# A causal convolution followed by an ELU feed-forward block: the tap band read unreversed from DRAM, an earlier halo memset, and a weight chunk copied inside SBUF

## The chip, the cores and the metric

The kernel runs on one core of one Trainium2 chip. The metric is the device time of one execution in microseconds (us), and smaller is better. Beside it there is one profiled execution, whose trace gives the start and length of every instruction, the releases of semaphores and the DMA records. TensorE is called PE here, VectorE DVE, ScalarE ACT, GpSimd POOL and SyncE SP, as in the profile.

## What is computed

The input `x` is 8 sequences of 4096 tokens of 192 channels. Each of the 8 heads (24 channels each) has 7 taps; the taps go through a softmax and then form a causal convolution along the sequence. The result goes through a two-layer block with an ELU between the layers.

```python
w = np.exp(weight - weight.max(-1, keepdims=True)); w /= w.sum(-1, keepdims=True) + 1e-9
x_pad = np.concatenate([np.zeros((B, 6, D)), x], axis=1)       # six zero tokens before each sequence
out = np.einsum('hk,bskhg->bshg', w, x_unf)                      # x_unf: 7-token windows of x_pad
h = out.reshape(32768, 192) @ w_in                               # 192 x 2048
g = np.where(h > 0, h, np.exp(np.minimum(h, 0)) - 1)
y = g @ w_out                                                    # 2048 x 192
```

## The kernel before, in words

The 32768 tokens are cut into 32 supers of 1024 tokens, four to a sequence. For every super, 16 steps (`q`, one per 128 columns of `w_in`) are made, 512 steps `n` in all. A step has two halves `u` (512 tokens each), which sit in the two 64-row halves of the PE array.

For each step and half, PE makes three matmuls into a PSUM bank of `H` (line 751: `w_in` against `att`, the convolved tokens), ACT takes the exponential into `E` (543), POOL clamps it (471), DVE forms `gT` as the maximum of `E - 1` and `H` and so frees the bank (612). Later PE makes the second product from `gT` and `w_out` (785). The bank pool for `H` has six places, so PE can be three steps ahead of DVE and no more. An order of all PE instructions is written out by the planner at the top (`put`, `steps`), with assumed costs; the other engines walk through the same list.

The convolution of a super is done on PE too (line 729), as matmuls of tokens `xg` with a band matrix `Tm` (128 partitions, 8 heads, 128 columns) that holds the seven taps of a head along its diagonals. ACT evicts it to `csb` (521), and SP turns it into `att` by a DMA transpose (389). Super 0 takes another way at the start: its tokens are loaded in fp32, cast, transposed on PE and convolved with diagonal matrices `Dg` (580, 684), so that step 0 need not wait for the band. The matmuls for super 1 stand in the PE order at steps 7 to 10 (`EARLY_CONV`), those for super 2 from step 13. Short "warm" matmuls (701) stand beside steps 0 to 5.

The band is made as follows. DVE writes the softmaxed taps into eight rows `zt` of 128 elements (570). SP writes two zero rows (802) and these eight rows (807) into a DRAM tensor `conv_taps`, waits for both, and reads 128 partitions of 1024 elements from it, each partition one element further than the one before (811), into `Tr`. DVE then copies `Tr` with each head's 128 elements reversed into `Tm` (598). In the DVE program this copy stands ahead of the first `gT`, and in the PE program the first convolution matmul waits for it (`s_tm`), and for the two tokens loads of super 1 (`x_ready`).

POOL issues the large loads at the start, in this order (line 475 on): `w_in` columns 0 to 511 for both partition halves (the same rows go to partitions 0 to 63 and 64 to 127), columns 512 to 2047 for both halves, `xg` of super 1 in two parts, `w_out`, `xg` of super 2 in two parts. All of these cast fp32 to 16 bits on the way. `Q_PART` says which chunk's semaphore PE waits for at a step.

A sequence begins at every fourth super, and its first six rows of `xg` must be zero. `pad_x(s)` on POOL (409, 410) does that with a memset, two supers ahead, at step `X_PAD` = 8 of the super, ahead of that step's clamps. The convolution of super `s + 2` begins in the PE order at step 9 of super `s`.

Of the kernel before, what the change touches and what calls it, by code (L numbers as in the profile page):

```python
# [8 lines left out]
BF16 = mybir.dt.bfloat16  # L9
# [3 lines left out]
P = 128  # L13
HP = 64
FC = 128
D = 192
HEADS = 8
KSIZE = 7
CPH = 24
CW = 128  # L20
# [4 lines left out]
TAP = 6  # L25
# [9 lines left out]
    ((0, (0, 15, 8, 9)), (1, (6, 6, 7, 13))),  # L35
)
RUN = 4
WCOLS = ((0, 512), (512, 2048))
Q_PART = (0,) * 4 + (1,) * 12
WARM = (9, 1)  # L40

CONV_AT = ((0, 1, 1, 0), (4, 1, 1, 1), (9, 2, 0, 0), (12, 2, 0, 1))
# [4 lines left out]
QUAD = 4  # L47
XTW = 136
HALO = 2
X_PAD, X_COPY, X_LOAD = 8, 3, 15  # L50
X_LATE = (13, 18)


def bass_lightweight_conv__then__act_elu_kernel(
# [94 lines left out]
    for n in range(NP):  # L149
        s, i = divmod(n, NQ)  # L150
# [64 lines left out]
            t, half = divmod(n_half - 1, 2)  # L215
            previous[n_half // 2, n_half % 2, 0, g] = (t, half, 0, g)

    taps = nc.dram_tensor("conv_taps", ((HEADS + 2) * CW,), BF16).ap()

    xb = nc.dram_tensor("x_cast", (NT, D), BF16).ap()  # L220

    with ExitStack() as stack:
        def sbuf(name, shape, dt):
            return stack.enter_context(nc.sbuf_tensor(name, shape, dt))
# [4 lines left out]
        def sema(name):  # L229
            return stack.enter_context(nc.semaphore(name))  # L230
# [9 lines left out]
        whe = sbuf("whe", [HEADS, KSIZE], FP32)  # L240
# [1 line left out]
        whr = sbuf("whr", [HEADS, 1], FP32)  # L242
        sel = sbuf("sel", [HEADS, P], BF16)
        xg = sbuf("xg", [P, NXB, 2 * WPG, D], BF16)
        Tr = sbuf("Tr", [P, HEADS, CW], BF16)
        Tm = sbuf("Tm", [P, HEADS, CW], BF16)
        csb = sbuf("csb", [P, 2, 3 * 2 * WPG * HP], BF16)
        att = sbuf("att", [P, 2, 3, WPG * TOK], BF16)
        w_in = sbuf("w_in", [P, 3, FF], BF16)
# [4 lines left out]
        zt = sbuf("zt", [HEADS, CW], BF16)  # L254
        xf = sbuf("xf", [P, 2, QUAD, D], FP32)
        zw = sbuf("zw", [P, GS], BF16)
        scr = sbuf("scr", [P, 2], FP32)
        H = psum("H", [P, 3, 2 * GS])
        ops = psum("ops", [P, 2, GS])

        s_w = [sema(f"s_w{i}") for i in range(3)]
        s_wd = sema("s_wd")
        s_xl = [sema(f"s_xl{i}") for i in range(2)]
        s_xh = sema("s_xh")
        s_xha = sema("s_xha")
        s_wp = sema("s_wp")
        s_wb = sema("s_wb")
        s_tm = sema("s_tm")
        s_xb = [sema(f"s_xb{i}") for i in range(2)]
        s_xq = [[sema(f"s_xq{i}_{g}") for g in range(2)] for i in range(NXB)]  # L270
        s_id = sema("s_id")
# [23 lines left out]
        s_band = sema("s_band")  # L295
# [98 lines left out]
        @block.gpsimd  # L394
        def _gpsimd(g: bass.BassGpSimd):
            W = Waits(g)

            def load_x(s, part):
                g.dma_start(  # L399
                    xg[:, s % NXB, WPG * part : WPG * (part + 1), :],  # L400
                    bass.AP(
                        tensor=x_flat.tensor,
                        offset=(s * SUP + GS * part - PAD) * D,
                        ap=[[D, P], [TOK * D, WPG], [1, D]],
                    ),
                ).then_inc(s_x[s % NXB][part], 16)

            def pad_x(s):
                x_ready(W, s, 0)
                g.memset(xg[0:PAD, s % NXB, 0, :], 0.0).then_inc(s_z)  # L410

            def copy_x(s):
                W(s_cv, 4 * (s - NXB - 1) + 1)
                if s == NXB + 1:
                    g.dma_start(  # L415
                        xb[s * SUP - 8 : s * SUP, :], x_flat[s * SUP - 8 : s * SUP, :]
                    ).then_inc(s_xb[s % 2], 16)
                g.dma_start(  # L418
                    xb[s * SUP : (s + 1) * SUP, :].rearrange("(p t) d -> p (t d)", p=P),
                    x_flat[s * SUP : (s + 1) * SUP, :].rearrange("(p t) d -> p (t d)", p=P),  # L420
                ).then_inc(s_xb[s % 2], 16)

            def load_w_in(k, halves):
                c0, c1 = WCOLS[k]
                for r in halves:
                    g.dma_start(  # L426
                        w_in[HP * r : HP * (r + 1), :, c0:c1],
                        moe_w_in.rearrange("(p j) f -> p j f", j=3)[:, :, c0:c1],
                    ).then_inc(s_w[k], 16)

            W(s_one, 1)
            g.affine_select(
                out=ident[:],
                in_=ident[:],
                pattern=[[-1, P]],
                compare_op=ALU.is_equal,
                fill=0.0,
                base=0,
                channel_multiplier=1,
            ).then_inc(s_id)  # L440
            g.affine_select(
                out=sel[:].rearrange("p (r h c) -> p r h c", r=2, h=HEADS),
                in_=sel[:].rearrange("p (r h c) -> p r h c", r=2, h=HEADS),
                pattern=[[0, 2], [-1, HEADS], [0, 8]],
                compare_op=ALU.is_equal,
                fill=0.0,
                base=0,
                channel_multiplier=1,
            ).then_inc(s_id)
            W(s_wd, 16)  # L450
            load_w_in(0, (0, 1))
            load_w_in(1, (0, 1))
            load_x(1, 0)
            load_x(1, 1)
            g.dma_start(
                w_out.rearrange("p (q r) d -> p q (r d)", r=RUN),
                moe_w_out.rearrange("(q p r) d -> p q (r d)", p=FC, r=RUN),
            ).then_inc(s_w[2], 16)
            load_x(2, 0)
            load_x(2, 1)  # L460
            for n in range(NP):
                s, i = divmod(n, NQ)
                if i == X_PAD and s + 2 < NS and (s + 2) % SPB == 0:
                    pad_x(s + 2)
                if i == X_COPY and s and s + 3 < NS:
                    copy_x(s + 3)
                if n == X_LATE[0]:
                    copy_x(3)
                for u in range(2):
                    W(s_exp, 2 * n + u + 1)  # L470
                    g.tensor_scalar(  # L471
                        out=E[:, n % NE, u, :],
                        in0=E[:, n % NE, u, :],
                        scalar1=1.0,
                        scalar2=0.0,
                        op0=ALU.min,
                        op1=ALU.max,
                    ).then_inc(s_clp)
# [72 lines left out]
        def _vector(v):  # L551
            W = Waits(v)
# [16 lines left out]
            W(s_v, 4)  # L569
            v.tensor_scalar(  # L570
                out=zt[:, TAP : TAP + KSIZE],
                in0=whe[:],
                scalar1=whr[:, 0:1],
                scalar2=None,
                op0=ALU.mult,
# [4 lines left out]
            v.tensor_tensor(  # L580
                Dg[:, 1:8, :],
                mask[:, :].unsqueeze(1).to_broadcast([P, KSIZE, HP]),
                H[:, 2, 0:KSIZE].unsqueeze(2).to_broadcast([P, KSIZE, HP]),
                ALU.mult,
            ).then_inc(s_D)
            W(s_tp, 3)
# [7 lines left out]
            v.tensor_copy(  # L594
                att[:, 0, 2, GS // 2 : GS], H[:, 1, GS : GS + GS // 2]
            ).then_inc(s_hd)
            W(s_band, 48)
            v.tensor_copy(Tm[:], Tr[:, :, ::-1]).then_inc(s_tm)  # L598
            for x_, op in enumerate(steps):
                if x_ in stops:  # L600
                    acc = acc_of(op)
# [3 lines left out]
                elif op[0] == "h" and op[3] == 2:  # L605
                    n, u = op[1:3]
                    s, q = divmod(n, NQ)
                    if s >= NG3:
# [5 lines left out]
                        in0=E[:, n % NE, u, :],  # L614
# [7 lines left out]
        def _tensor(pe):  # L622
            W = Waits(pe)
# [51 lines left out]
            for j in range(3):  # L675
# [3 lines left out]
                for k in range(KSIZE + 1):  # L679
                    shift, i = divmod(k - PAD, QUAD)  # L680
                    step = 2 * XTW if i < 2 else 1 - 2 * XTW
                    for r in range(2):
# [5 lines left out]
                                tensor=whole.tensor,  # L688
                                offset=whole.offset,
                                ap=[whole.ap[0], [step, 2], [1, P]],  # L690
# [7 lines left out]
            for x_, op in enumerate(steps):  # L698
# [10 lines left out]
                elif op[0] == "c":  # L709
# [3 lines left out]
                    if hh == 0 and second:  # L713
                        W(s_cs, 2 * m + b + 1)
                    elif hh == 0:
                        if m == 0:
                            W(s_tm, 1)
                            if b:
                                W(s_cv, 1)
                        for part in range(2):  # L720
                            x_ready(W, s, part)
                        W(s_z, z_need[s])
                        if m >= OPS_CONV:
                            wait_bank()
                        elif m:
                            W(s_ce, 2 * (m - 1) + b + 1)
                    n1 = BN // HB
                    h = 4 * u + HB * b + hh
# [12 lines left out]
                elif op[0] == "h":  # L741
                    _, n, r, j = op
                    s, q = divmod(n, NQ)
# [1 line left out]
                        W(s_ha, (1, 1, 2)[j])  # L745
                        W(s_hd, (0, 1, 2)[j])
                    if j == 0:
                        W(s_w[Q_PART[q]], 32)
                        W(s_att[s % 2], 16 * ((s + 1) // 2))
                        wait_bank()  # L750
                    ins = pe.matmul(  # L751
# [13 lines left out]
                else:  # L765
                    _, item, rt, g = op
                    t, half, q, kb, turned = item
                    acc = acc_of(op)
                    W(s_w[2], 16)
                    W(s_tt, 2 * (NQ * t + q) + g + 1)  # L770
                    at_end = acc[:2] == (last, 1)
                    if x_ in begins:
# [24 lines left out]
        def _sync(sy):  # L797
            W = Waits(sy)
# [1 line left out]
            load_first(sy, 1)  # L800
            W(s_zw, 1)
            sy.dma_start(
                bass.AP(tensor=taps.tensor, offset=0, ap=[[(HEADS + 1) * CW, 2], [1, CW]]),
                zw[0:2, 0:CW],
            ).then_inc(s_band, 16)
            W(s_wp, 1)
            sy.dma_start(
                bass.AP(tensor=taps.tensor, offset=CW, ap=[[CW, HEADS], [1, CW]]), zt[:, :]
            ).then_inc(s_band, 16)
            W(s_band, 32)  # L810
            sy.dma_start(
                Tr[:, :, :].rearrange("p h e -> p (h e)"),
                bass.AP(tensor=taps.tensor, offset=TAP + 1, ap=[[1, P], [1, HEADS * CW]]),
            ).then_inc(s_band, 16)

            def load_cast(s):
                W(s_cv, 4 * (s - NXB))
# [16 lines left out]
            for x_, op in enumerate(steps):  # L834
                if op[0] == "h" and op[2:] == (0, 0):
                    s, i = divmod(op[1], NQ)
# [52 lines left out]
```

## Time and profile before

| | |
|---|---|
| median of three runs | 734.09 us (733.89 to 734.24) |
| profiled execution, whole / its span | 735.32 us / 733.0 us |
| PE busy | 717.8 us (98% of the span) |
| ACT, DVE, POOL busy | 657.2, 652.7, 630.5 us (90, 89, 86%) |
| first matmul of step 0 (751) | starts at 10.95 us |
| `Tr` read (811), issue to the last of its landings | 7.27 to 16.29 us |
| first `gT` (612) | starts at 16.65 us |
| first convolution matmul (729) | starts at 23.74 us |
| first second-layer matmul (785) | starts at 32.12 us |
| halo memsets (410) | 7, of 0.25 us each |

PE is busy in every slice of the page but the first, so a microsecond in which PE stands still late in the kernel is a microsecond of the total. In the first 32 us this isn't so yet: PE has no second-layer work, and the time of a step is that of the slowest engine in the ring PE, ACT, POOL, DVE, or of a load. Times in the text are counted from the start of the span.

### The profile page before, as it was taken

To read this page: it belongs to the slowest core of one execution; us is meant where nothing else is said; L and a number is where in the kernel's file an instruction comes from. 1 tells how busy PE (TensorE), PEld (TensorE's weight loads), DVE (VectorE), ACT (ScalarE), POOL (GpSimd) and SP (SyncE) were. 2 spreads that over 40 slices of the span, in tenths; PEclk is the share of its full clock that TensorE was granted. 3 is DMA by queue.
4 is the path that set the end of the run, shared out by engine and by line. 5 is a ranking of instruction groups with operands and counts; after the bars stand their busy time and mean duration, and the time that the engine had idled before them with its cause. 6 is when DMAs were issued, how large, how long until landed. Compare 5 with 4: busy or idle time off the path is not lost.

```text
span 733.0 us, 28722 instructions
## 1 busy us (share of the span) xinstructions
PE 717.8 (98%) x11866; PEld 640.9 (87%) x11866; DVE 652.7 (89%) x1044; ACT 657.2 (90%) x1286; POOL 630.5 (86%) x1076
## 2 busy tenths in 40 slices
PE   6999999999999999999999999999999999999997
PEld 3598999888999898998998989998898989898997
DVE  3899899999999899998999999999899999999994
ACT  4898999989999999999999989999999989999993
POOL 6889888888888898888898888898888888888893
PEclk9899999999999999999999999999999999999999
DMA  9755334445445544335554445464345453532212
GB/s 177 110 93 114 70 93 115 103 81 98 86 94 114 91 92 106 78 94 114 89 95 99 86 94 114 84 100 97 81 99 115 80 104 86 100 93 70 57 36 66
DMA packets 128959, 69.12 MB, mean 94 GB/s; under 512 B 93932, under 2 KB 127596, under 8 KB 128364
## 3 DMA queue, kind: packets, MB, share of 16 engines
q1 hardware_dynamic: 123596, 52.04, 30.3%
q0 software_dynamic: 4944, 14.75, 14.4%
q8 instruction: 93, 1.52, 0.9%
q10 hardware_dynamic: 288, 0.49, 0.2%
q14 instruction: 38, 0.31, 0.1%
HBM read 43.51 MB, written 36.57 MB: 109 GB/s over the span
## 4 chain that ended last, share of the span: by engine, by line
PE 94%; DMA 2%; ACT 2%; POOL 1%; issue 1%; DVE 0%; ACTq 0%
PE ops L785 50%; PE H L751 40%; PE H L729 3%; DMA Tr<-conv_taps 1%; ACT E L543 1%; POOL E L471 1%; PE H L785 1%; DMA conv_taps<-zt 0%; DVE gT L612 0%; POOL xg L410 0%; ACT L484 0%; ACT csb L521 0%; PE ops L701 0%; POOL x_cast L415 0%; POOL x_cast L418 0%
## 5 line engine op out<-in xcount | busy, mean ns | idle before, releaser
L612 DVE SCALAR_TENSOR_TENSOR gT<-E,H 128x512 f16<-128x512 f32 x1024 | 646.5, 683 | 59.9 <-POOL E L471 51.2
L471 POOL TENSOR_SCALAR E<-E 128x512 f32<-128x512 f32 x1024 | 607.0, 616 | 90.2 <-ACT E L543 86.4
L543 ACT ACTIVATE E<-H 128x512 f32<-128x512 f32 x1024 | 566.8, 613 | 58.3 <-PE H L751 53.8
L751 PE MATMUL H<-att,w_in 64*128 64x512 bf16 x3072 | 612.2, 379 | 5.1 <-DVE gT L612 4.3
L785 PE MATMUL ops<-w_out,gT 64*128 64x192 f16 x8064 | 594.6, 243 | 0.0
L785 PEld LDWEIGHTS ops<-w_out,gT 64*128 64x128 f16 x8064 | 523.7, 94 | 41.6 <-PE ops L785 26.2
L751 PEld LDWEIGHTS H<-att,w_in 64*128 64x128 bf16 x3072 | 293.1, 111 | 20.3 <-DVE gT L612 7.6
L729 PE MATMUL H<-xg,Tm 64*128 64x240 bf16 x480 | 87.6, 262 | 4.1 <-POOL xg L410 3.8
L521 ACT ACTIVATE csb<-H 128x480 bf16<-128x480 f32 x120 | 70.5, 588 | 0.0
L513 ACT ACTIVATE osb<-ops 128x384 f32<-128x384 f32 x125 | 61.1, 488 | 7.3 <-PE ops L785 5.7
L729 PEld LDWEIGHTS H<-xg,Tm 64*128 64x128 bf16 x480 | 39.7, 94 | 19.0 <-issue 6.6
L418 POOL DMA_DIRECT2D x_cast<-in_x_dram x29 | 15.7, 540 | 0.0
L785 PE MATMUL H<-w_out,gT 64*128 64x192 f16 x128 | 6.5, 243 | 0.0
L785 PEld LDWEIGHTS H<-w_out,gT 64*128 64x128 f16 x128 | 5.8, 94 | 0.0
L701 PE MATMUL ops<-zw 64*128 64x512 bf16 x12 | 5.7, 502 | 0.0
L598 DVE COPY Tm<-Tr 128x1024 bf16<-128x1024 bf16 x1 | 0.4, 427 | 5.7 <-DMA Tr<-conv_taps 5.7
L640 PE MATMUL ops<-zw 128*128 128x512 bf16 x9 | 4.0, 631 | 1.3 <-DVE zw L553 1.3
L604 DVE COPY osb<-ops 128x384 f32<-128x384 f32 x1 | 0.6, 558 | 4.3 <-PE ops L785 4.3
L640 PEld LDWEIGHTS ops<-zw 128*128 128x128 bf16 x9 | 1.2, 142 | 3.2 <-issue 1.9
L399 POOL DMA_DIRECT2D xg<-in_x_dram x4 | 3.5, 877 | 0.0
L729 PE MATMUL ops<-xg,Tm 64*128 64x240 bf16 x16 | 3.0, 265 | 0.4 <-ACT csb L521 0.3
L426 POOL DMA_DIRECT2D w_in<-in_moe_w_in_dram x4 | 2.7, 682 | 0.3 <-DMA wh<-in_weight_dram 0.3
(50 smaller groups left out, 30.6 us busy)
## 6 DMA issues: line engine op xcount, KB each, us to landing
out_dram<-osb SPq DMA_DIRECT2D x126, 192.0 KB, 3.2
x_cast<-in_x_dram POOLq DMA_DIRECT2D x29, 384.0 KB, 5.1
xg<-x_cast SPq DMA_DIRECT2D x58, 192.0 KB
xg<-x_cast SPq DMA_DIRECT2D x58, 26.2 KB
w_in<-in_moe_w_in_dram POOLq DMA_DIRECT2D x2, 576.0 KB, 11.7
xg<-in_x_dram POOLq DMA_DIRECT2D x4, 240.0 KB, 15.3
w_out<-in_moe_w_out_dram POOLq DMA_DIRECT2D x1, 768.0 KB, 16.4
att<-csb SPq DMA_TRANSPOSE x31, 5.9
```

Source lines behind the costliest of these rows:

```text
L399: g.dma_start(xg[:, s % NXB, WPG * part : WPG * (part + 1), :], bass.AP(tensor=x_flat.tensor, offset=(s * SUP + GS * part - PAD) * D, ap=[ ...
L418: g.dma_start(xb[s * SUP : (s + 1) * SUP, :].rearrange("(p t) d -> p (t d)", p=P), x_flat[s * SUP : (s + 1) * SUP, :].rearrange("(p t) d - ...
L471: g.tensor_scalar(out=E[:, n % NE, u, :], in0=E[:, n % NE, u, :], scalar1=1.0, scalar2=0.0, op0=ALU.min, op1=ALU.max,).then_inc(s_clp)
L513: a.activation(*out_pieces(acc), ACT.Copy).then_inc(s_oev)
L521: return a.activation(csb[:, s % 2, :].rearrange("p (j v h i) -> p h j v i", j=3, v=2 * WPG, h=HEADS)[:, h0 : h0 + HB], bank_of(("c", m, b ...
L543: a.activation(E[:, n % NE, u, :], bank_of(op[:3]), ACT.Exp).then_inc(s_exp)
L612: v.scalar_tensor_tensor(out=gT[:, s % NG3, q, u, :], in0=E[:, n % NE, u, :], scalar=1.0, in1=bank_of(op[:3]), op0=ALU.subtract, op1=ALU.m ...
L640: pe.matmul(ops[:, 0, :], zw[:, 0:P], zw[:], start=True, stop=True)
L701: pe.matmul(ops[:, 1 - rt, :], zw[HP * rt : HP * (rt + 1), 0:P], zw[HP * rt : HP * (rt + 1), :], start=True, stop=True, tile_position=(HP ...
L729: ins = pe.matmul(bank_of(op[:3])[:, n1 * hh : n1 * (hh + 1)], Tm[HP * rt : HP * (rt + 1), h, :], xg[HP * rt : HP * (rt + 1), s % NXB, :, ...
L751: ins = pe.matmul(bank_of(op[:3]), w_in[HP * r : HP * (r + 1), j, RUN * FC * (q // RUN) + q % RUN : RUN * FC * (q // RUN + 1) : RUN,], att ...
L785: ins = pe.matmul(to[:, d0 : d0 + D], gT[HP * rt : HP * (rt + 1), t % NG3, q, g, t0 : t0 + P], w_out[HP * rt : HP * (rt + 1), q, :], start ...
```

## The change

- The taps are written into `zt` in reversed order, and `Dg` reads them back in reversed order. `conv_taps` holds the zero rows and tap rows twice, one copy behind the other. The band is read straight into `Tm`, and each partition starts one element before the one before it; partitions 64 to 127 read from the second copy. `Tr`, its copy on DVE and `s_tm` are gone; PE waits for the band's own semaphore.
- `X_PAD` is 5 in place of 8.
- `w_in` comes in three chunks. Columns 1024 to 2047 are loaded from DRAM for partitions 0 to 63 only, ahead of columns 512 to 1023; SP then copies them inside SBUF to partitions 64 to 127, behind the band read. At steps 8 to 15 PE waits for the load (rows 0 to 63) or the copy (rows 64 to 127).

```diff
-WCOLS = ((0, 512), (512, 2048))
-Q_PART = (0,) * 4 + (1,) * 12
+WCOLS = ((0, 512), (512, 1024), (1024, 2048))
+Q_PART = (0,) * 4 + (1,) * 4 + (2,) * 8
-X_PAD, X_COPY, X_LOAD = 8, 3, 15
+X_PAD, X_COPY, X_LOAD = 5, 3, 15
...
-    taps = nc.dram_tensor("conv_taps", ((HEADS + 2) * CW,), BF16).ap()
+    taps = nc.dram_tensor("conv_taps", (2 * (HEADS + 2) * CW,), BF16).ap()
...
             load_w_in(0, (0, 1))
+            load_w_in(2, (0,))
             load_w_in(1, (0, 1))
...
-                in0=whe[:],
+                in0=whe[:, ::-1],
...
-                H[:, 2, 0:KSIZE].unsqueeze(2).to_broadcast([P, KSIZE, HP]),
+                H[:, 2, KSIZE - 1 :: -1].unsqueeze(2).to_broadcast([P, KSIZE, HP]),
...
-            W(s_band, 48)
-            v.tensor_copy(Tm[:], Tr[:, :, ::-1]).then_inc(s_tm)
...
-                            W(s_tm, 1)
+                            W(s_band, 48)
...
-                        W(s_w[Q_PART[q]], 32)
+                        if Q_PART[q] < 2:
+                            W(s_w[Q_PART[q]], 32)
+                        else:
+                            W(s_wc if r else s_w[2], 16)
...
-                bass.AP(tensor=taps.tensor, offset=0, ap=[[(HEADS + 1) * CW, 2], [1, CW]]),
-                zw[0:2, 0:CW],
+                bass.AP(tensor=taps.tensor, offset=0, ap=[[(HEADS + 2) * CW, 2], [(HEADS + 1) * CW, 2], [1, CW]]),
+                zw[0:2, 0 : 2 * CW].rearrange("p (a e) -> p a e", a=2),
...
-                bass.AP(tensor=taps.tensor, offset=CW, ap=[[CW, HEADS], [1, CW]]), zt[:, :]
+                bass.AP(tensor=taps.tensor, offset=CW, ap=[[CW, HEADS], [(HEADS + 2) * CW, 2], [1, CW]]),
+                zt[:, :].unsqueeze(1).to_broadcast([HEADS, 2, CW]),
...
-                Tr[:, :, :].rearrange("p h e -> p (h e)"),
-                bass.AP(tensor=taps.tensor, offset=TAP + 1, ap=[[1, P], [1, HEADS * CW]]),
+                Tm[:, :, :].rearrange("p h e -> p (h e)"),
+                bass.AP(tensor=taps.tensor, offset=CW + TAP + KSIZE - 1, ap=[[(HEADS + 2) * CW - HP, 2], [-1, HP], [1, HEADS * CW]]),
             ).then_inc(s_band, 16)
+
+            c0, c1 = WCOLS[2]
+            W(s_w[2], 16)
+            sy.dma_start(w_in[HP:P, :, c0:c1], w_in[0:HP, :, c0:c1]).then_inc(s_wc, 16)
```

More of the change, by code (lines that the diff above doesn't have):

```diff
@@ L244, in bass_lightweight_conv__then__act_elu_kernel @@
         xg = sbuf("xg", [P, NXB, 2 * WPG, D], BF16)
-        Tr = sbuf("Tr", [P, HEADS, CW], BF16)
         Tm = sbuf("Tm", [P, HEADS, CW], BF16)
@@ L259, in bass_lightweight_conv__then__act_elu_kernel @@
         ops = psum("ops", [P, 2, GS])
-        s_w = [sema(f"s_w{i}") for i in range(3)]
+        s_w = [sema(f"s_w{i}") for i in range(4)]
+        s_wc = sema("s_wc")
         s_wd = sema("s_wd")
@@ L267, in bass_lightweight_conv__then__act_elu_kernel @@
         s_wb = sema("s_wb")
-        s_tm = sema("s_tm")
         s_xb = [sema(f"s_xb{i}") for i in range(2)]
@@ L457, in _gpsimd @@
                 moe_w_out.rearrange("(q p r) d -> p q (r d)", p=FC, r=RUN),
-            ).then_inc(s_w[2], 16)
+            ).then_inc(s_w[3], 16)
             load_x(2, 0)
@@ L768, in _tensor @@
                     acc = acc_of(op)
-                    W(s_w[2], 16)
+                    W(s_w[3], 16)
                     W(s_tt, 2 * (NQ * t + q) + g + 1)
```

## The prediction

> **What bounds the kernel now.** I read the page's busy shares first (PE 98%), then the waits of the whole run for what stops PE, then the chain of waits and equal stretches for what each stop costs. Two places stand out. The waits, with columns engine, line, who was waited for, total us, times, longest:
>
> ```profile
> PEld H L751 <- DVE gT L612: 7.6, 8, 4.2
> ...
> DVE Tm L598 <- DMA Tr<-conv_taps: 5.7, 1, 5.7
> ...
> PE H L729 <- POOL xg L410: 3.8, 7, 0.6
> ```
>
> The first two belong together: DVE stands before the band copy, so it frees no bank of `H`, so PE stands. The third is the halo memset, seven times.
>
> The chain of the start (start, length, what) and stretches cut at PE's clock changes (length, busy us with instruction counts, granted clock, DMA share, GB/s):
>
> ```profile
> 3.61 3.64 DMA conv_taps<-zt
> ...
> 7.27 9.02 DMA Tr<-conv_taps
> ...
> 16.31 0.43 DVE Tm L598
> 16.74 0.61 DVE gT L612
> ...
> 17.39 1.64 PE H L751 x5
> ```
>
> ```profile
> 13.28:16.69 3.41, 0.43 (x5) 0.00 (x0) 0.38 (x2) 1.56 (x4) 2.71 (x5) 1.00 1.30 199
> 16.69:20.10 3.41, 2.71 (x13) 1.62 (x15) 3.41 (x7) 1.20 (x2) 0.53 (x1) 0.50 1.32 206
> 20.10:23.52 3.42, 3.42 (x20) 2.37 (x17) 2.70 (x5) 2.39 (x4) 2.43 (x5) 0.50 1.38 196
> 23.52:26.93 3.41, 3.26 (x31) 1.84 (x28) 3.04 (x5) 3.08 (x7) 3.04 (x6) 1.00 0.32 38
> ```
>
> PE stands from 13.7 to 17.39, then runs 6.8 us at half clock, and reaches the first convolution at 23.74. The token loads of super 1 landed at 18.35 and 19.68 by the landing records, so here they delay nothing.
>
> Around a halo memset, the chain, and stretches of one super each (the first and last hold a memset):
>
> ```profile
> 71.42 0.62 POOL E L471
> 72.03 0.20 POOL xg L410
> 72.23 0.24 issue
> 72.48 0.26 PE H L729
> ```
>
> ```profile
> 141.27:164.00 22.73, 22.18 (x375) 19.83 (x372) 20.46 (x33) 20.57 (x41) 19.73 (x35) 1.00 0.47 93
> 164.00:185.83 21.83, 21.83 (x371) 19.68 (x368) 20.10 (x33) 20.30 (x41) 19.35 (x34) 1.00 0.50 96
> 185.83:207.74 21.91, 21.91 (x372) 19.78 (x370) 20.19 (x33) 20.37 (x41) 19.45 (x34) 1.00 0.49 97
> 207.74:229.65 21.91, 21.91 (x372) 19.79 (x370) 20.19 (x33) 20.38 (x41) 19.44 (x34) 1.00 0.49 97
> 229.65:252.38 22.73, 22.18 (x375) 19.82 (x372) 20.47 (x33) 20.57 (x41) 19.73 (x35) 1.00 0.48 93
> ```
>
> PE is full but for 0.55 us in each super with a memset.
>
> **What the Trainium skill says.** "TensorE: Matmul & The Clock Gate", Part 1: the clock halves after about one idle window of 3.4 us in a free-running grid, and returns after a busy one. The trace agrees: two stretches of 3.41 us at 0.50, after one that PE spent almost wholly idle. "DMA: Bandwidth & Descriptors", Why a DMA increments its semaphore by 16: a DMA issued by SP runs on k engines, the largest number up to 16 that divides the slowest dimension of both access patterns, and the other 16 - k counts are written at once. The trace agrees: the band's semaphore shows 28 increments, 2 + 1 for the two zero rows, 8 + 1 for the eight tap rows, 16 for the 128-partition read. Same page, Queues, rings and completion order: an engine takes turns between the queues that have work, and one queue keeps its order. The trace agrees: from 11 to 14 us 116 band rows (2 KB, mostly 96 ns) and 145 `w_in` rows (3 KB, 248 ns) went side by side, about one to one.
>
> **Part 1, the halo.** Four supers take 22.73 + 21.83 + 21.91 + 21.91 = 88.38 us, against 4 x 21.91 = 87.64 without the memset: 0.74 each (the stall of 0.55 and what follows it). Seven times: 5.2 us, at least 7 x 0.55 = 3.8. Is it hidden at step 5? The memset stands ahead of clamps that start at 68.30 there (72.20 now), after 0.25 us in which POOL is idle: it fits. The rows it writes landed at 59.97 (first case) and 146.9 (second, clamps at 156.7), so POOL won't block; if it did, PE would run dry after its three banks, some 4 us. The convolution is at 72, 3.6 us after the new place. I take -5.0.
>
> **Part 2, the band and the loads, up to the first convolution.** DVE's first clamped `E` is there at 13.1 (POOL starts it at 12.49, 0.62 us), so without the copy `gT` starts 3.55 us sooner and PE doesn't stop at 13.7. A step then costs two `gT`, 1.28 us; PE needs the bank freed by the first half of step 4, and so stands before the first convolution at 13.1 + 4 x 1.28 + 0.64 = 18.9. What does it wait for there?
>
> The new read's source has an outermost dimension of 2, its target 128. By the skill's rule k is 2: 64 rows on each of two engines where there were 8. No DMA before shows this shape with this size, so I work out the load on these two engines and bound it.
> - Start: issued near 7.3 to 7.6 as now (the tap writes have one more 256-byte row of 31 ns per engine). The first rows moved 3.5 us after issue, behind a `w_in` transfer; now 10.0 to 10.8.
> - `w_in` work per engine after chunk 0: before 24 rows of 3 KB, 24 x 248 = 5.95 us. After: 12 of 2 KB (173 ns, between the 97 of 1 KB rows and 248) and 24 of 1 KB (97 unhindered, 146 at the pace seen from 4 to 8 us): 4.4 to 5.6, so 0.4 to 1.6 less.
> - The band: 64 x 96 - 8 x 96 = 5.4 us more.
> - The SBUF copy: 12 rows of 2 KB, 12 x 96 = 1.15 us more, on these engines behind the band.
>
> Sum for the two: 5.4 + 1.15 less 0.4 to 1.6, so 5.0 to 6.2, say 5.5 more. The second token load's typical engines landed at 17.4 to 18.2, so on these two it lands near 23.1 (22.4 to 24.4). Five of 16 engines ran nearly 2 us later (19.0 to 19.7); if one of them is among the two, near 24.9 (24.0 to 25.9). The band itself is done earlier, as it takes turns with loads that end later. With even odds the convolution begins at 24.0 (22.4 to 26).
>
> The stall from 18.9 is hidden by nothing. `w_in` columns 512 to 1023, now third, land at about 15 to 17.6, wanted at step 4 (15.0); that only moves part of the same stall forward. The copied half chunk, wanted a step after the convolution begins, lands with the tokens. `w_out` (23.4 now) and super 2's tokens (26.0) come about 5 us later on the two engines, 28.5 and 31; wanted at 32.0 and 31.9. SP's next job is the transpose at 30.73: nothing is queued behind the copy.
>
> After the convolution begins, ACT is the bound (busy 6.02 of the 6.07 us from 26.93). It now starts step 7's first exponential at about 24.9; after, 0.5 us behind the convolution, 1.0 at half clock (a stall of 5 us may hold a whole idle window). So break-even is a convolution at 24.4, or 23.9 at half clock; with 24.0 I get -0.4 or +0.1. I take -0.2, with the ends -2 (22.4) and +2.1 (26 at half clock).
>
> The reversed operands of DVE (0.22 and 0.61 us) keep their sizes. If a reversed read cost double, `Dg` still has 1.1 us before PE's use at 7.37, and the taps add 0.22 to the band's start. I take 0. The copy's 0.43 us is in the 3.55.
>
> **Sum.** -5.0 - 0.2 = -5.2: span 733.0 to 727.8, that execution 735.32 to 730.1, and, as it lies 1.2 above the median, 728.9 for the median.
>
> **The rivals.**
> - *The start keeps its gain*: the read is spread over 16 engines. Then the tokens land near 19.7 as now, the convolution starts by 20.2 (20.7 for the exponential against 24.9): -4.2, total 734.09 - 5.0 - 4.2 = 724.9. For it: nothing in the trace but that this shape is new. Against: the 2 + 1 and 8 + 1 increments. 0.13.
> - *One of the two engines is a late one and the clock halves*: start +1.5 to +3.5, total 730.6 to 732.6. Five late of 16 speak for it; that the stall is shortened by the step-4 wait, against. 0.20.
> - *Another wait takes the memset's place*: at the convolution of a new sequence PE would wait as long for a bank or a load. Total 733.9, no change. The other three supers show no wait at that place. 0.06.
> - *The band rows go slowly on two engines*: slower than before. Single rows took up to 294 ns in crowded moments. It decides where the start loses more than 5.0 + 1.5: 6.8 us over 64 rows, from about 205 ns a row. At 250: 64 x 154 ns = 9.9, total about 738.5. Against: 96 ns was the usual length with 16 engines at it. 0.08.
>
> **How the numbers follow.** The forecast case, start within -1.5 and +1.5, halo -5.0, has 0.53 and 727.4 to 730.6. A difference of 0.2% is 1.5 us and is about what can be told from no change. Faster is 0.53 + 0.13 + 0.20 = 0.86, the same 0.06, slower 0.08. The range 725.0 to 732.6 leaves out the lower half of the first rival and the last two, 0.2 in all.
>
> **What would show it.** Halo: the wait of 729 on the memset gone, all supers at 21.9. Start: no PE stop at 13.7; first `gT` at 13.1; a PE stop of 4 to 6 us that ends with the first convolution at 23 to 25; 2 + 1 increments for the band; its rows moving until after 19 us. Wrong would be: the band landed by 15 (then 724.9), or the convolution after 28.

## The result and the profile after

The changed kernel takes 731.54 us in the median (731.19 to 731.63), against 734.14 before (now the median of four runs, with a later one): a ratio of 0.9964 with a 95% interval of 0.9947 to 0.9981. The forecast was 728.9, so about half of the forecast gain (2.6 of 5.2 us) came. That is outside the forecast case's own 727.4 to 730.6 and inside the wider range, which reached up to 732.6 for a rival. The profiled execution took 731.6 us, with a span of 729.1.

The waits of the whole run after (engine, line, who was waited for, total us, times, longest). The convolution's line is now 727, the first product's 752, the second's 786:

```profile
PEld H L752 <- DVE gT L610: 5.7, 13, 0.8
...
PEld ops L727 <- issue: 5.4, 2, 5.2
PE ops L727 <- DMA xg<-in_x_dram: 5.0, 1, 5.0
...
PE H L727 <- DVE gT L610: 0.3, 1, 0.3
```

The wait of 729 on the halo memset (3.8 us, 7 times) is gone, and so is the long stop behind DVE. In its place PE waits 5.0 us, once, for the tokens of super 1. The chain of waits at the start says the same (start, length, what):

```profile
5.77 0.90 POOL xg L398
6.67 17.07 DMA xg<-in_x_dram
23.74 0.14 issue
23.87 0.36 PE ops L727
```

A load of 240 KB takes 17 us. The reason is in the landing records of the trace; each landing is one DMA engine's increment of a semaphore (times in us):

```
                          before                     after
band read                 16 landings, 13.9-16.3     2 landings, 20.83 and 21.45
tokens of super 1, part 2 16 landings, 17.4-19.7     14 landings, 14.8-17.0, and 22.92 and 23.74
copy inside SBUF          -                          14 landings, 19.9-21.2, and 22.75 and 23.41
```

On 14 engines the tokens are there by 17.0; on the two others, where the band read is, they come 6 to 7 us later. The stretches after, cut in part where the clock changes (length, busy us with counts for PE, PEld, DVE, ACT and POOL, granted clock as a share of PE's full one, DMA share, GB/s):

```profile
15.10:18.50 3.40, 3.21 (x23) 1.23 (x22) 3.40 (x7) 2.94 (x6) 3.40 (x7) 1.00 1.18 252
18.50:21.67 3.17, 0.42 (x4) 0.11 (x1) 2.94 (x5) 1.08 (x2) 1.95 (x4) 1.00 1.31 221
21.67:25.08 3.41, 1.21 (x9) 0.95 (x10) 0.00 (x0) 0.00 (x0) 0.00 (x0) 0.50 0.63 82
25.08:28.50 3.42, 3.36 (x22) 2.02 (x19) 1.28 (x2) 2.76 (x6) 1.73 (x3) 0.50 0.17 24
28.50:33.00 4.50, 3.92 (x28) 1.50 (x25) 3.85 (x6) 4.50 (x10) 3.65 (x8) 1.00 0.03 3
```

DVE now runs through the time in which it stood before the band copy. But PE stops at 18.9, five microseconds later than it did before, and for longer, and comes back at half clock. The first second-layer matmul starts at 33.22 us, against 32.12 in the profile before.

Two stretches of one super each, of which the first ends and the second begins just ahead of a halo memset's place, show what the memset now costs:

```profile
134.50:156.40 21.90, 21.90 (x373) 19.75 (x370) 20.18 (x33) 20.36 (x42) 19.37 (x34) 1.00 0.45 97
156.40:178.30 21.90, 21.90 (x373) 19.75 (x369) 20.17 (x33) 20.37 (x42) 19.57 (x35) 1.00 0.50 97
```

PE has no gap in either. The 0.2 us more of POOL in the second is the memset, and nobody waits for it.

### The profile page after: what moved, and what is told of

It reads as the page before. It is cut to its first block, busy times and chain, and to the rows that moved or that the text cites. A ratio compares the mean times of both kernels' runs of the same rounds, so it can differ in the third digit from the quotient of the medians.

```text
span 729.1 us, 28725 instructions
## 1 busy us (share of the span) xinstructions
PE 715.9 (98%) x11866; PEld 638.9 (88%) x11866; DVE 651.5 (89%) x1043; ACT 656.2 (90%) x1286; POOL 629.0 (86%) x1077
## 4 chain that ended last, share of the span: by engine, by line
PE 95%; DMA 2%; POOL 1%; ACT 0%; DVE 0%; issue 0%
PE ops L786 51%; PE H L752 40%; PE H L727 3%; DMA xg<-in_x_dram 2%; PE H L786 1%; POOL E L471 0%; POOL w_in L425 0%; ACT E L543 0%; DVE gT L610 0%; PE ops L727 0%; POOL xg L398 0%; ACT csb L521 0%; POOL x_cast L414 0%; POOL x_cast L417 0%; POOL sel L440 0%
## 5 line engine op out<-in xcount | busy, mean ns | idle before, releaser
L727 PEld LDWEIGHTS ops<-xg,Tm 64*128 64x128 bf16 x16 | 1.5, 114 | 6.8 <-issue 5.4
L699 PE MATMUL ops<-zw 64*128 64x512 bf16 x12 | 4.2, 379 | 0.0
## 6 DMA issues: line engine op xcount, KB each, us to landing
w_out<-in_moe_w_out_dram POOLq DMA_DIRECT2D x1, 768.0 KB, 19.9
```

Of the source, the lines that this page charges most:

```text
L699: pe.matmul(ops[:, 1 - rt, :], zw[HP * rt : HP * (rt + 1), 0:P], zw[HP * rt : HP * (rt + 1), :], start=True, stop=True, tile_position=(HP ...
L727: ins = pe.matmul(bank_of(op[:3])[:, n1 * hh : n1 * (hh + 1)], Tm[HP * rt : HP * (rt + 1), h, :], xg[HP * rt : HP * (rt + 1), s % NXB, :, ...
```

## The experiments

The theory was: the halo gains what was forecast; the start loses because the band read sits on two engines and holds back, on these two, all that is queued there. The first rival was that the new mix of loads (columns 512 to 1023 third, a copy beside the tokens) is what makes the tokens late. A second question was what the loss of the start is made of: the clock, or the empty ring of PE, ACT, POOL and DVE. All ratios below are against runs of the kernel before on the same chip. Three chips were used, on which the kernel before took 733.99, 734.37 and 734.36 us, so a difference between two experiments, where it is taken from their times, can be off by about 0.4 us for the chip alone.

**The halo alone**, on the kernel before:

```diff
-X_PAD, X_COPY, X_LOAD = 8, 3, 15
+X_PAD, X_COPY, X_LOAD = 5, 3, 15
```

> The kernel before with the halo memset at step 5 in place of 8, and nothing else. If the memset's wait is worth what the equal stretches showed (0.74 us in each of seven supers), the time is 734.1 - 5.0 = 729.1, the start is as before (first convolution matmul at 23.7 us), and every super takes 21.9 us. If the halo is worth less and the start of the changed kernel is even with before, as predicted, the time is near 730.3 (-3.8, the bare stalls).

Measured: 728.89 us against 733.99, ratio 0.9927 (0.9912 to 0.9942). That is -5.1 us, the full 0.74 a piece and not the bare stalls. Supers 2 to 29 take 21.91 to 21.93 us each, those with a memset too (22.64 in the kernel before). In its profile the start is the old one (DVE waits 5.3 us for `Tr`), but the first convolution is at 22.28 and the first second-layer matmul at 30.94, 1.2 us earlier than in the profile of before, with nothing changed there. PE has one stretch at half clock here, where the profile of before has two:

```profile
14.04:17.45 3.41, 0.34 (x3) 0.15 (x3) 1.54 (x3) 0.99 (x3) 2.13 (x4) 1.00 1.39 192
17.45:20.86 3.41, 3.41 (x19) 1.29 (x18) 3.41 (x7) 1.79 (x3) 1.34 (x3) 0.50 1.23 209
20.86:24.27 3.41, 3.07 (x30) 1.46 (x26) 3.09 (x6) 3.18 (x7) 3.17 (x6) 1.00 1.29 166
```

This matters below.

**The start alone**, the changed kernel with the memset back at step 8:

```diff
-X_PAD, X_COPY, X_LOAD = 5, 3, 15
+X_PAD, X_COPY, X_LOAD = 8, 3, 15
```

> The changed kernel with the halo memset back at step 8: the start of the changed kernel alone. If the start loses what the first second-layer matmul shows (33.22 against 32.12 us), the time is 734.1 + 1.1 = 735.2. If the start is even and the halo is worth only 3.8, it is near 734.1 to 735.3 less 1, that is 734.1.

Measured: 736.71 us, ratio 1.0031 (1.0021 to 1.0041): the start loses 2.7 us, more than twice the 1.1 that the two profiles show. The waits of this kernel hold both stops side by side:

```profile
PE ops L727 <- DMA xg<-in_x_dram: 5.1, 1, 5.1
...
PE H L727 <- POOL xg L409: 3.8, 7, 0.5
```

The edits add up: -5.1 + 2.7 = -2.4, and the whole change gave -2.6.

**The band on sixteen engines**: sixteen copies of the tap rows, each read by a block of 8 partitions, the rest as changed. That gives an outermost dimension of 16.

```diff
-    taps = nc.dram_tensor("conv_taps", (2 * (HEADS + 2) * CW,), BF16).ap()
+    taps = nc.dram_tensor("conv_taps", (16 * (HEADS + 2) * CW,), BF16).ap()
...
-                bass.AP(tensor=taps.tensor, offset=CW + TAP + KSIZE - 1, ap=[[(HEADS + 2) * CW - HP, 2], [-1, HP], [1, HEADS * CW]]),
+                bass.AP(tensor=taps.tensor, offset=CW + TAP + KSIZE - 1, ap=[[(HEADS + 2) * CW - 8, 16], [-1, 8], [1, HEADS * CW]]),
```

The two writes into `conv_taps` change likewise (16 zero-row pairs from `zw[0:16]`, each tap row written 16 times).

> The changed kernel with sixteen copies of the tap rows in DRAM in place of two, so that the source's outermost dimension is 16 and each block of 8 partitions reads its own copy; the rest as changed. Theory (the read is confined to two engines, and what is queued on these two is late): the band's semaphore gets 16 increments for the read, the band lands before 16 us, the tokens of super 1 by 18, the first convolution starts near 19.0, without half clock afterwards; the time is 731.5 - 5 to 6.4, so 725.1 to 726.5. Rival (the new mix of loads is what is late: columns 512 to 1023 third, the copy inside SBUF beside the tokens): the tokens still come after 22 and the time stays within 1 us of 731.5.

Measured: 726.13 us, ratio 0.9889 (0.9872 to 0.9906), 5.4 below the changed kernel and faster than both. The band lands at 13.7 to 15.7, the tokens by 18.54 (18 had been expected), the first convolution starts at 19.18 and the clock is 1.00 throughout. The rival falls: the load mix is the same here. From the chain of waits of this kernel (start, length, what):

```profile
11.37 0.38 PE H L752
...
13.55 7.28 DVE gT L610 x12
20.83 0.01 issue
20.83 0.59 ACT E L543
21.43 0.46 ACT csb L521
```

Here the start has no load on its chain after 11.4 us; DVE, step by step, is what sets it. The waits show the copied half chunk as a small one: `PEld` 0.5 us, once.

**PE kept busy in its stop**, the changed kernel with twenty matmuls on zeros ahead of the first convolution's wait:

```diff
+FILL = 20
...
                         if m == 0:
+                            if b == 0:
+                                for _ in range(FILL):
+                                    pe.matmul(ops[:, 0, :], zw[:, 0:P], zw[:], start=True, stop=True)
                             W(s_band, 48)
```

> The changed kernel with twenty more matmuls of 128x512 on zeros ahead of the first convolution's wait (some 4.3 us at full clock), which write a bank that the convolution writes over afterwards: PE isn't idle while it waits, so the clock should stay full. If the start's loss of 1.1 us against before is the half clock after the stop (0.50 from 21.7 to 28.5 us), the first exponential after the stop comes about 0.5 us after the convolution begins and not 1.45, and the time falls by about 1 to 730.5. If it is the empty ring of PE, ACT, POOL and DVE, the time stays at 731.5.

Measured: 729.72 us, ratio 0.9937 (0.9923 to 0.9952): 1.8 below the changed kernel, for work that computes nothing. From PE's instructions in order (start, length, line, what, idle before):

```profile
19.58 4.26 PE L718 MATMUL ops<-zw 128*128 128x512 bf16 x19 [0.16 <-issue]
24.85 0.26 PE L731 MATMUL ops<-xg,Tm 64*128 64x240 bf16 x1 [1.00 <-DMA xg<-in_x_dram]
```

The clock is 1.00 throughout. The first exponential comes 0.84 us after the convolution, not the 0.5 expected, but 0.6 sooner than in the changed kernel (1.45). The tokens came 1.0 us later in this profile (24.7), and still the first second-layer matmul is at 32.97 against 33.22. From the first convolution to it there are 8.1 us, against 9.35 in the changed kernel. So by the profiles 1.2 us of the start's loss is the half clock after the stop; by the medians the filling is worth 1.8.

**The load as before**, the band on two engines: the changed kernel with `WCOLS`, `Q_PART`, the loads and the waits of before, and without the copy.

```diff
-            load_w_in(2, (0,))
...
-            W(s_w[2], 16)
-            sy.dma_start(w_in[HP:P, :, c0:c1], w_in[0:HP, :, c0:c1]).then_inc(s_wc, 16)
```

> The changed kernel with w_in loaded as before (two chunks, both partition halves from DRAM, no copy inside SBUF); the band is still read by two engines. Theory (the two engines' own work sets the first convolution): they have 0.4 to 1.6 us more of w_in and 1.15 less of the copy, so the convolution starts at 23.1 to 24.3 us and the time is 730.8 to 732.0. Rival (the split load or the copy is what holds the start back): the convolution starts by 21 and the time falls below 729.5.

Measured: 730.38 us, ratio 0.9943 (0.9929 to 0.9956). The convolution starts at 23.19, within what was expected; the time is 0.4 under the expected stretch, and not down to the rival's. PE now stops twice, at step 4 and at the convolution, and the second stop is the shorter for it (waits, columns as above):

```profile
PE ops L726 <- DMA xg<-in_x_dram: 3.6, 1, 3.6
PEld H L751 <- DMA w_in<-in_moe_w_in_dram: 1.6, 1, 1.6
```

In this profile PE also has one half-clock stretch (24.07 to 27.48) in place of two. The convolution is 0.7 us earlier than in the changed kernel, and the way from it to the first second-layer matmul is 0.7 shorter (8.7 us).

**The load as before, the band on sixteen engines:** both edits above.

> Sixteen tap copies (read on 16 engines) and w_in loaded as before in two chunks. The second chunk's last landing was at 17.4 to 17.6 us in the runs with this load, and step 4 wants it at 15.0: PE stops there for about 2.5 us, so the first convolution starts near 21.4 in place of 19.2, and the time is near 728.3. If the split of the load is worth nothing once the band is on 16 engines, it is 726.1 as with the split.

Measured: 728.12 us, ratio 0.9915 (0.9902 to 0.9928), 2.0 above the sixteen-engine kernel with the split load. The stop at step 4 is where it was expected (PE's instructions in order):

```profile
14.68 0.38 PE L751 MATMUL H<-att,w_in 64*128 64x512 bf16 x1
17.10 0.61 PE L751 MATMUL H<-att,w_in 64*128 64x512 bf16 x1 [2.05 <-DMA w_in<-in_moe_w_in_dram]
```

So the split of the load is worth 2.0 us where the band is on sixteen engines. With the band on two it gains nothing: 731.54 with it against 730.38 without. That it costs those 1.2 us isn't shown, as the intervals of the two ratios overlap and the two profiles differ in their half-clock stretches.

**Four engines:** four copies of the tap rows, `[[(HEADS + 2) * CW - 32, 4], [-1, 32], [1, HEADS * CW]]`, the rest as changed.

> Four copies of the tap rows, so the read is on four engines with 32 rows each; the rest as changed. The other engines have the tokens at 14.8 to 17.0; 32 rows of 96 ns add 3.1 us, so the last token lands at 18 to 20.1, the convolution starts at 19.2 to 20.2 (PE arrives at 18.9) and the time is 726 to 727.3. If the loss with two engines is of another kind than rows in line (a slow path for this shape), four engines lose as much: 730 to 731.5.

Measured: 727.92 us, ratio 0.9907 (0.9894 to 0.9921), 0.6 over the expected stretch. Four landings of the second token part are late (21.05 to 21.16), the other 12 by 17.5, and PE waits for the late ones:

```profile
21.30 0.26 PE L727 MATMUL ops<-xg,Tm 64*128 64x240 bf16 x1 [2.30 <-DMA xg<-in_x_dram]
```

The last token is 1.1 us over the 18 to 20.1 expected. Two things were missing from that sum. The copy's 12 rows are on these engines too (12 x 96 = 1.15 us), and the band's rows took 124 ns in the mean here, not 96 (32 x 28 = 0.9 us). With both the sum gives 20 to 22; how much is due to each isn't shown. The loss shrinks with the rows in line on an engine:

```
engines of the band   rows on each   last token   first convolution   median us
 2                    64             23.74        23.87               731.54
 4                    32             21.16        21.30               727.92
16                     8             18.54        19.18               726.13
```

**DVE's copy moved back**, on the kernel before, with the memset at step 5; nothing of the band or the loads is changed:

```diff
-            W(s_band, 48)
-            v.tensor_copy(Tm[:], Tr[:, :, ::-1]).then_inc(s_tm)
             for x_, op in enumerate(steps):
...
                     ).then_inc(s_tt)
+                    if (n, u) == (2, 1):
+                        W(s_band, 48)
+                        v.tensor_copy(Tm[:], Tr[:, :, ::-1]).then_inc(s_tm)
```

> The kernel before with the memset at step 5 and with DVE's reversing copy moved behind the second gT of step 2; the band, its 16-engine read and all loads as before. If DVE's place in line is all that held PE in the kernel before, PE no longer stops at 13.7; it stops at step 4 for the second w_in chunk (15.0 to 17.5) and starts the convolution near 21.4: near 728.3, that is 0.6 below the memset edit alone, about as with 16 engines and the whole load. If the copy's 0.43 us in the ring counts in full, near 728.7.

Measured: 728.01 us, ratio 0.9913 (0.9898 to 0.9927). It is as fast as the sixteen-engine band with the whole load (728.12), so what the reversed read gains over before is DVE's place in line, and moving that one copy gains it as well. Whether the moved copy with the split load would reach the 726.1 of the sixteen-engine kernel was not run. From DVE's instructions in order:

```profile
13.06 3.68 DVE L610 SCALAR_TENSOR_TENSOR gT<-E,H 128x512 f16<-128x512 f32 x6 [2.87 <-POOL E L471]
16.65 0.69 DVE L620 COPY Tm<-Tr 128x1024 bf16<-128x1024 bf16 x1
17.27 1.27 DVE L610 SCALAR_TENSOR_TENSOR gT<-E,H 128x512 f16<-128x512 f32 x2
```

**The kernel before with PE kept busy in its own stop**, for the 1.2 us that its profile had over others with the same start:

```diff
                     if j == 0:
+                        if n == 3 and not filled:
+                            filled.append(1)
+                            for _ in range(16):
+                                pe.matmul(ops[:, 0, :], zw[:, 0:P], zw[:], start=True, stop=True)
                         W(s_w[Q_PART[q]], 32)
```

(`filled` is a list that is empty at the start of the PE program.)

> The kernel before with sixteen more matmuls of 128x512 on zeros (3.5 us at full clock) at the place where PE stops at 13.7 us, ahead of step 3, so that PE isn't idle while DVE stands before the band copy. If the time of the kernel before depends on where its stop of 3.7 us falls in the grid of the clock gate (25 timed runs: those with a granted clock of 0.995 or 0.994 at 734.7 to 736.1, the others at 733.4 to 735.5), the clock stays full, the runs come together within 0.8 us and the median is at the lower end of before, 733.0 to 733.6. If the clock has no part in it, the median is 734.2 and the runs scatter over 2 us or more as before.

Measured: 733.05 us against 734.36, ratio 0.9981 (0.9973 to 0.9989), 15 runs from 732.48 to 733.93 (a wider spread than the 0.8 expected), with a granted clock of 0.998 to 1.000. The stop is filled from 14.11 to 17.74 (start, length, what):

```profile
14.11 3.63 PE L751 MATMUL ops<-zw 128*128 128x512 bf16 x16
```

The clock is 1.00 throughout, DVE's first `gT` is at 16.65 as in the profile of before, and the first second-layer matmul is at 30.71 against 32.12. So the clock has its part in the time of before, about 1.3 us in the median. Of 45 executions of the kernel before whose clock is listed, 13 at 0.995 had a median of 735.38 us, and 32 above that a median of 733.99. Its profiled execution was one of the 13.

## Why the prediction was right and wrong

**Right: the halo.** Forecast -5.0, measured -5.1. The measure by equal stretches (0.74 us per memset, more than the stall of 0.55) was the right one, and the place at step 5 is hidden as argued.

**Right: the mechanism of the start.** The band's semaphore got 2 + 1 increments for the read. `gT` starts at 12.98 (13.1), PE doesn't stop at 13.7 but at 18.9 (18.9), and the convolution starts at 23.87 (24.0). That the last number fits so well is in part luck: 24.0 was the middle between 23.1 for typical engines and 24.9 for a late one, and what came was typical engines, 0.6 later than the sum. On the two engines the band rows took turns with what POOL had queued there: from 12 to 16 us 11 to 16 band rows a microsecond moved on the two, that is 182 ns a row on each at first and 125 at the end. A band row in turn with a 1 KB `w_in` row makes 96 + 98 = 194 ns, and with a token row 96 + 51 = 147. One term came out kinder than forecast: columns 512 to 1023 had landed by 15.12, not up to 17.6, so step 4 waited 0.5 us only.

**Wrong: what a convolution at 24 means, by two terms.** The forecast for the start was -0.2; measured are +2.7 (the start alone; 1.5 to 3.0 by the interval of its ratio) and, by the difference of the changed kernel and the halo alone, +2.65.

The first term is the step "0.5 us behind the convolution, 1.0 at half clock". The first exponential came 1.45 us after the convolution, at 25.33, where the step gives 24.9 (23.87 + 1.0); at full clock, with PE kept busy, it came 0.84 us after. And "after the convolution begins, ACT is the bound" holds at full clock, not at half. In the stretch from 25.08 to 28.50 PE is busy 3.36 of 3.42 us and ACT 2.76; at 0.50 PE was the bound until 28.5. From the convolution to the first second-layer matmul there were 9.35 us, against 8.4 in the profile before and 8.1 with PE kept busy. Against the profile before, this makes +1.1.

The second term is the step "as it lies 1.2 above the median": I carried that distance over to the changed kernel. It isn't a fixed cost of profiling. The profile of before was an execution with two half-clock stretches, and most executions of before have less: the halo kernel, with the same start, had one, and was 1.2 us further on by the first second-layer matmul (0.3 of this is a band that landed sooner, `gT` at 16.38 against 16.65). The kernel before with its stop filled had none, and was 1.4 further on with its `gT` at 16.65. After the change the stop of 5 us brings two such stretches in both profiles of this start (6.83 us at 0.50), and the four timed runs all show 0.995. So the profiled execution after (731.6) stands at its median, and the 1.2 us that I took off isn't there; -0.2 + 1.3 + 1.2 = +2.3, and 0.4 of the 2.7 stay unassigned, though 2.3 lies within the interval above.

**The rivals.** The case "one of the two engines is a late one and the clock halves" had 730.6 to 732.6, and the time fell there, but for half of its reason only, which is luck: the clock halved, while neither of the two engines was a late one (22.92 and 23.74, against 23.1 forecast for typical engines and 24.9 for a late one). The sixteen-engine case, 724.9, is what the kernel with sixteen copies shows, and it took 726.13 though its convolution was at 19.18 (20.2 in that case). The second term is in that forecast too: its gain of 4.2 was read in the profile that stood 1.2 above the median, and taken off the median; from 735.32 it gives 726.1. That the band's rows are slow on two engines is not so (96 ns a row), and no other wait took the memset's place (supers 2 to 29 take 21.91 or 21.92 us each).

## What to carry to other kernels

Look at the outermost dimension of a DMA, not only at its bytes: here a read cut in 2, 4 or 16 there had 2, 4 or 16 landings, one for each engine it ran on. The price of the two was paid by loads of another queue that use the same engines and were done on the others almost seven microseconds before (17.0 against 23.7). Where a profile shows PE stopped for a few microseconds, price the restart at half clock as well, with PE as the bound; and where the stop is near the length of the clock's grid (3.41 us here), one profile is one draw, so compare timed medians before carrying its distance to the median over. Before a rewrite removes a wait, see whether moving the one instruction that stands in line does the same.

## What the runs showed that I had not expected

- The clock halved without a wholly idle grid stretch. In the start the clock record stays at one value for 3.41, 6.83, 10.24, 13.65 or 17.07 us at a time, always a multiple of 3.41. In the eleven traces, cut on this grid over the first 45 us, there are ten in which PE was busy 10 to 41% of the time, and each was followed by 0.50 (in two the clock was at half already). The least busy one that was followed by full clock had 49% (the kernel before with its stop filled, 8.2 to 11.6). Once at half clock, a stretch 80% busy (the profile of before, 16.7 to 20.1) didn't bring the full clock back, and stretches of 98% and more did. The Trainium skill ("TensorE: Matmul & The Clock Gate", Part 1) speaks of an idle window; here, by measurement, 40% busy was idle enough. What the share is in general isn't shown. From the stretches of the sixteen-engine kernel with the whole load:

```profile
13.75:17.16 3.41, 1.36 (x10) 0.33 (x10) 3.41 (x7) 1.92 (x4) 3.12 (x6) 1.00 1.36 221
17.16:20.58 3.42, 3.42 (x18) 1.38 (x20) 1.24 (x3) 1.36 (x3) 1.19 (x2) 0.50 1.25 209
```

- The copy inside SBUF, 384 KB, was issued at 12.65 us and landed at 19.9 to 21.2 even on the 14 engines without band rows. I had put it beside the tokens, with its landing at theirs. On these engines its rows moved from about 16 us, beside `w_out` rows.
- The issue of the reversed read took SP 0.66 us, and that of the copy 0.68, against 0.35 for the read before.
